# An attention and gated feed-forward kernel: the planner's release times of the output-weight preparation, 40 units earlier

## The chip, the cores and the metric

The kernel runs on one core of one Trainium2 chip. The metric is device time in microseconds (us) for one execution, measured without the profiler; the profile shows another, single execution. Engines go by the profile's names: PE is the TensorE matmul, PEld its weight load, DVE the VectorE, ACT the ScalarE, POOL the GpSimd, SP the SyncE, whose queue issues nearly every transfer (DMA).

## The reference

For 8 batches and 8 heads (576 positions, 64 wide) windowed attention is computed; its output, as 4608 tokens of 512 features, goes through a gated feed-forward layer with 1536 hidden features.

```python
scores = np.where((rel >= 0) & (rel < 128), scale * q @ k.T + slope * -abs(rel), -1e9)
x = (softmax(scores) @ v)                        # as 4608 x 512 tokens
gate = 1.0 / (1.0 + np.exp(-(x @ w_gate)))
val = x @ w_val
return (gate * val @ w_out).astype(np.float32)
```

## The kernel before

Every engine's program is written out by a planner. `Graph.add` takes an operation with its engine, an assumed cost, the keys that it reads and writes, a priority `want` and a `release`, before which the planner doesn't start it. `Graph.order` plays a list schedule on these assumed costs and emits the operations sorted by their planned start. On the chip nothing is timed: each engine runs its list in this order and waits on semaphores. So a `release` sets only where an operation stands in the lists, in the planner's own microseconds.

The work has three stages. First, attention of 32 head pairs, and the first four blocks of 128 hidden features for the first 2048 or so tokens (`ffn`, L646). Second, the **seven-product stage** (`ffn2`, L780): the gate and value products of a block as a 2x2 block matrix product with seven products in place of eight (Winograd's form). A *chunk* is one block of 128 hidden features for one group of tokens. It has seven products of six matmuls each, in the order 0, 3, 4, 1, 5, 2, 6, on three PSUM banks `bx`, `by`, `bz`. Products 4, 5 and 6 accumulate on `bx`, product 2 on `bz`, after ACT has copied out what stood there: to `low` (L201), or for product 3 to the chunk's buffer `later_hs` (L201, `p5`), and DVE has added (L787) and gated (L795). The finished chunk is stored to DRAM (`hid`). The stage runs first over groups of 2 x 384 tokens (24 chunks), then over three groups of 2 x 512 tokens (24 chunks). Third, the output product (`last`, L910), by the same form, for all five groups; it reads `hid` back (`rows_*`), builds sums of it (`csum`, L865) and splits them into pairs (`duo`).

The weights are split into a high and a low float32r part. For the output weights this is `prepare_o(n)`, n = 0 to 5: two loads of 512 KB (`wraw`), decoding (ACT L337, DVE L338 and L341), differences of the quarter blocks (L209, L210) in `tt`, splitting into `wg0` and `wtmp0`, `wtmp1` (L201 or L202, then L210), and four stores to DRAM (`stash_o`, two of 128 KB and two of 768 KB). Later `fetch_o` reads each `stash_o` back into the space of a weight tile of the second stage (`wo`, two of 896 KB), when that tile has been used for the last time.

The six preparations share `wraw`, `tt`, `wtmp0` and `wtmp1`. These last two lie in the memory of the third and fourth `later_hs` buffers:

```python
six = lambda p: T(moe, f"wtmp{p}", [P, 6, 2 * P], F32R, tag=f"h{3 + p}")
def hs(e, name="later_hs"):
    return T(moe, f"{name}{e}", [P, 2, NB] if name == "later_hs" else [P, NB], F32, tag=f"hs{e}" if e < 2 else f"h{e + 1}")
```

In most of the stage the chunks take turns on `later_hs0` and `later_hs1`. In the last group of 512 (`ends`) they take turns on all four, so there the third chunk of the group writes `later_hs2` where `wtmp0` was, and the fourth `later_hs3` where `wtmp1` was:

```python
if ends:
    for p in range(2):
        follow([("wtmp", p)] + [("hs", 2 + p, j) for j in range(2)])
...
e = turns[0] % (4 if ends else 2)
```

`rows_hs0` and `rows_h3` of the last stage are loaded into the memory of `later_hs0` and `later_hs2`, once the store of the chunk there has landed. All these transfers stand in one list on SP, which issues them in order and waits for each one's condition before the next.

When a preparation may be planned is set by two constants, `OUT0` and `OSTEP`:

```python
for n in range(NFC // 2):
    prepare_o(n, 2.0e6 + n, OUT0 + OSTEP * n)
```

Of the kernel before, what the change touches and what calls it, by code (L numbers as in the profile page):

```python
# [39 lines left out]
KEEP2 = 3  # L40
NPB, NST, NPT, NBOTH = 8, 9, 3, 2
P0, PSTEP = 120.0, 56.0
OUT0, OSTEP = 470.0, 36.0
TRI = 3
VDELAY = 1
VHEAD = 11
# [1048 lines left out]
```

## Time and profile before

| | |
|---|---|
| time, three runs | 987.4, 987.62, 988.33 us; median 987.62 us |
| the profiled execution's own time | 988.12 us |
| its span, first to last instruction | 986.4 us |
| mean granted TensorE clock | 0.994 |
| busy: PE, DVE, ACT, POOL | 98%, 80%, 52%, 13% |
| seven-product stage, L780 | about 304 to 724 us of the span |
| output product, L910 | 723.96 us to the end |

The table says which engine is busy, not which wait ends last; that is read in the rows below. The 1.72 us between span and own time lie before the first and behind the last instruction.

### The profile page before, as it was taken

Reading aid. Unit: us, or ns where it says so; the run is one execution under the profiler, and the core shown is the slowest. Engines: PE = TensorE matmul, PEld = TensorE weight load, DVE = VectorE, ACT = ScalarE, POOL = GpSimd, SP = SyncE. Lnnn points to the kernel's source line nnn. Section 1 sums busy time; section 2 is a strip of 40 time slices with the busy share of each in tenths; the row PEclk is TensorE's granted clock in tenths of the full one; section 3 lists DMA queues with packets and bytes.
Section 4 is the critical chain, followed back from the end, with each engine's and each line's share of the span. In section 5 each row is a group of like instructions: output and inputs, shape, how many; then the busy total and the mean of one; then the engine's idle time right before and its main releaser. Section 6 shows DMA issues by size and latency. Waiting matters only on the chain.

```text
span 986.4 us, 18539 instructions
## 1 busy us (share of the span) xinstructions
PE 962.8 (98%) x6592; PEld 835.3 (85%) x6592; DVE 793.7 (80%) x2014; ACT 509.4 (52%) x1324; POOL 126.8 (13%) x221
## 2 busy tenths in 40 slices
PE   8999999999999999999999999995999999999998
PEld 7677888888879999999988888884888888889998
DVE  8999989898978998867866867755498977877783
ACT  8999877878745454334533533522344433333341
POOL 3434343343320000000020000000000000000000
PEclk9999999999999999999999999997999999999999
DMA  8778768877645444233382373393986435162601
GB/s 299 259 235 305 234 214 293 276 230 243 206 135 177 141 141 135 98 139 134 131 302 118 124 292 150 107 355 119 393 294 194 157 109 192 60 197 80 193 17 64
DMA packets 82077, 186.03 MB, mean 189 GB/s; under 512 B 7744, under 2 KB 36800, under 8 KB 81984
## 3 DMA queue, kind: packets, MB, share of 16 engines
q1 hardware_dynamic: 81840, 184.71, 54.2%
q8 instruction: 52, 0.85, 0.4%
q14 instruction: 41, 0.34, 0.1%
q10 hardware_dynamic: 144, 0.13, 0.0%
HBM read 122.95 MB, written 61.87 MB: 187 GB/s over the span
## 4 chain that ended last, share of the span: by engine, by line
PE 64%; DVE 2%; DMA 1%; issue 0%; ACT 0%; ACTq 0%
PE mm L780 38%; PE mm L910 26%; DMA hid<-later_hs 0%; DVE wbits L341 0%; DVE mm L787 0%; DMA stash_o<-wtmp 0%; DVE w2s L210 0%; DMA stash_o<-wg 0%; DVE later_hs L795 0%; DVE later_hs L787 0%; ACT low L201 0%; DVE wbits L338 0%; DVE wtmp L202 0%; DVE low L743 0%; DVE later_xr L743 0%
## 5 line engine op out<-in xcount | busy, mean ns | idle before, releaser
L780 PE MATMUL mm<-xc,w2s 128*128 128x384 f32 (+1 forms) x2016 | 408.1, 364 | 12.2 <-ACT later_hs L201 9.2
L780 PEld LDWEIGHTS mm<-xc,w2s 128*128 128x128 f32 x2016 | 365.5, 189 | 54.6 <-ACT later_hs L201 9.7
L910 PE MATMUL mm<-duo,wo 128*128 128x512 f32 (+1 forms) x1260 | 258.9, 367 | 0.0
L910 PEld LDWEIGHTS mm<-duo,wo 128*128 128x128 f32 x1260 | 229.3, 188 | 29.5
L646 PE MATMUL mm<-first,first 128*128 128x512 f32 x576 | 154.0, 406 | 1.7 <-DVE first L210 1.3
L646 PEld LDWEIGHTS mm<-first,first 128*128 128x128 f32 x576 | 102.0, 188 | 25.2 <-DVE first L210 2.9
L787 DVE TENSOR_TENSOR mm<-mm,low 128x384 f32<-128x384 f32 (+1 forms) x96 | 60.1, 628 | 66.0 <-PE mm L780 65.4
L791 ACT ACTIVATE sg<-mm 128x384 f32<-128x384 f32 (+1 forms) x96 | 52.2, 545 | 114.9 <-PE mm L780 65.1
L201 ACT COPY low<-mm 128x384 f32<-128x384 f32 (+1 forms) x94 | 50.2, 534 | 82.5 <-PE mm L780 70.8
L475 ACT ACTIVATE pb<-pb,st 128x128 f32<-128x128 f32 x216 | 84.5, 396 | 5.4 <-DVE st L471 5.1
L571 POOL TENSOR_SCALAR_AFFINE_SELECT pt<-early_h 128x384 f32<-128x384 f32 x96 | 51.7, 558 | 112.6 <-ACT early_h L201 102.3
L571 POOL TENSOR_SCALAR_AFFINE_SELECT pt<-early_xr 128x384 f32<-128x384 f32 x96 | 51.9, 563 | 52.0 <-ACT early_xr L201 48.3
L463 DVE COPY_PREDICATED mm<-early_h,mm 128x256 f32<-128x256 int32 (+1 forms) x144 | 50.1, 389 | 4.0 <-PE mm L446 3.8
L471 DVE CUSTOM_DVE_ANT_0 pb<-mm,early_h 128x128 f32<-128x128 f32 x216 | 51.0, 280 | 0.0
L517 PEld LDWEIGHTS mm<-pt,vr 64*64 64x64 f32 x924 | 37.5, 133 | 9.1 <-issue 3.5
L795 DVE SCALAR_TENSOR_TENSOR later_hs<-sg,later_hs 128x384 f32<-128x384 f32 (+1 forms) x48 | 31.5, 656 | 15.7 <-ACT sg L791 15.7
L201 ACT COPY later_hs<-mm 128x512 f32<-128x512 f32 (+1 forms) x45 | 24.1, 535 | 36.9 <-PE mm L780 20.8
L475 ACT ACTIVATION_READ_ACCUMULATOR pb<-pb,st 128x1 f32 x216 | 41.5, 192 | 0.0
L517 PE MATMUL mm<-pt,vr 64*64 64x192 f32 (+2 forms) x924 | 41.4, 285 | 0.0
L201 ACT COPY early_xr<-mm 128x384 f32<-128x384 f32 (+3 forms) x76 | 32.9, 446 | 14.0 <-PE mm L517 9.8
L787 DVE TENSOR_TENSOR later_hs<-mm,later_hs 128x384 f32<-128x384 f32 (+1 forms) x48 | 29.8, 620 | 11.6 <-ACT sg L791 5.3
L553 DVE TENSOR_SCALAR pb<-pb,st 128x128 f32<-128x128 f32 x162 | 38.2, 286 | 0.2
(138 smaller groups left out, 1222.3 us busy)
## 6 DMA issues: line engine op xcount, KB each, us to landing
hid<-later_hs SPq DMA_DIRECT2D x24, 512.0 KB, 4.6
wo<-stash_o SPq DMA_DIRECT2D x12, 896.0 KB, 7.7
vr<-in_v_dram SPq DMA_DIRECT2D x32, 288.0 KB, 4.8
hid<-later_hs SPq DMA_DIRECT2D x24, 384.0 KB, 2.8
stash_o<-wtmp SPq DMA_DIRECT2D x12, 768.0 KB, 4.1
wraw<-in_moe_w_gate_dram SPq DMA_DIRECT2D x16, 512.0 KB, 4.6
wraw<-in_moe_w_val_dram SPq DMA_DIRECT2D x16, 512.0 KB, 4.2
kr<-in_k_dram SPq DMA_DIRECT2D x11, 576.0 KB, 4.7
```

What stands on the lines that cost most here:

```text
L201: g.add("ACT", act_cost(n, psum), lambda: nc.scalar.copy(out(), src()), reads, writes, want, release=release, slack=slack, ways=[("DVE", d ...
L463: g.add("DVE", dve_cost((a1 - a0) * P, psum=True), lambda b=b, a0=a0, a1=a1: nc.vector.copy_predicated(quads(b)[:, a0:a1, 1:3], before[:, ...
L471: g.add("DVE", 0.21, lambda: nc.vector.tensor_tensor_reduce(pb()[:, e], sp[b][:, a, D:D + P], relm[u.p][:, w], op0=ALU.add, op1=ALU.min, s ...
L475: g.add("ACT", 0.39, lambda: nc.scalar.activation(pb()[:, e], pb()[:, e], AF.Exp, bias=st()[:, e:e + 1], scale=-1.0, accum_out=st()[:, 3 + ...
L517: nc.tensor.matmul(mm[WORK[h]][e * D:(e + 1) * D, a - e * S - cuts[h]:b - e * S - cuts[h]], vraw(u)[r * D:r * D + D, c], seen, start=first ...
L553: g.add("DVE", 0.19, lambda args=args: nc.vector.tensor_scalar_mul(*args()), [(kst, 6)], [(kpb, e)], want, port=True, ways=[("ACT", 0.3, F ...
L571: nc.gpsimd.affine_select(pt(u)[:, f0:f0 + 2 * n - 1:2, :], both(), [[0, n], step], cmp, 0.0, base=0, channel_multiplier=mult)
L646: nc.tensor.matmul(mm[s][:, 0:wd], w.tile(kind, wi, i)[:, c * P:(c + 1) * P], xpart(x, c)[:, 0:wd], start=(k == 0 and c == 0), stop=(k == ...
L780: nc.tensor.matmul(mm[b][:, 0:N2], w.tile2(i, wp)[:, wk, c * P:(c + 1) * P], combo(k, xp, N2)[:, c], start=(start and c == 0 and j == 0), ...
L787: g.add("DVE", dve_cost(N2, psum=True), lambda: nc.vector.tensor_tensor(o(), bk(b)(), a(), op=ALU.add), [("mm", b), *reads] if okeys else ...
L791: g.add("ACT", act_cost(N2, psum=True), lambda: nc.scalar.activation(sg[h](), bk(b)(), AF.Tanh, scale=0.5), [("mm", b)], [("sg", h)], F)
L910: nc.tensor.matmul(mm[b][:, 0:N2], wo2(2 * q + m, wp)[:, k, j * P:(j + 1) * P], duo(xp)[:, m], start=(k in (0, 3, 1) and q == 0 and m == 0 ...
```

## The change

One constant changes. The planner may start the six preparations at 430, 466, ... 610 of its own microseconds, where it could at 470, 506, ... 650. No operation is added or removed; their places in the lists change.

```diff
-OUT0, OSTEP = 470.0, 36.0
+OUT0, OSTEP = 430.0, 36.0
```

**SP, the end of the seven-product stage.** These rows stand in SP's list before, around the stores of the fifth and the loads and stores of the sixth preparation. `stash_o_113` is the fifth, `stash_o_114` the sixth; `wtmp_5938` is `wtmp0`; `hid_142` and `hid_137` are the stores of the first and second chunk of the last group, `hid_122` of the third.

```order
L206 DMA hid_142<-later_hs_4329 128x1024
L206 DMA stash_o_113<-wg_5876 128x256
L206 DMA stash_o_113<-wtmp_5938 128x1536
L206 DMA stash_o_113<-wtmp_5947 128x1536
L206 DMA wo_6926<-stash_o_110 128x1792
L206 DMA wo_6929<-stash_o_110 128x1792
L206 DMA hid_137<-later_hs_4357 128x1024
L206 DMA wraw_215<-in_moe_w_out_dram 128x1024
L206 DMA wraw_221<-in_moe_w_out_dram 128x1024
L206 DMA stash_o_114<-wg_5876 128x256 x2
L206 DMA stash_o_114<-wtmp_5938 128x1536
L206 DMA stash_o_114<-wtmp_5947 128x1536
```

The same place of the changed kernel, where `wtmp_5663` is `wtmp0`:

```order
L206 DMA hid_142<-later_hs_4329 128x1024
L206 DMA stash_o_114<-wtmp_5663 128x1536
L206 DMA stash_o_114<-wtmp_5673 128x1536
L206 DMA wo_6948<-stash_o_110 128x1792
L206 DMA wo_6951<-stash_o_110 128x1792
L206 DMA hid_137<-later_hs_4357 128x1024
L206 DMA wo_7014<-stash_o_111 128x1792
L206 DMA wo_7016<-stash_o_111 128x1792
```

Between the first two chunks' stores the sixth preparation's `wtmp` stores stand where the fifth's stood, and behind the second chunk's no preparation is left. The preparations two to five move in the same way, each about to where the one before it in number was.

**ACT, the place of the first preparation.** It stands in the last two groups of 384 now, where no preparation of output weights was. `low` and `later_hs` are the copies out of PSUM that PE waits for; `mm` is a bank.

```order
 L201 COPY later_hs_4357<-mm_74 128x384
 L201 COPY low<-mm_72 128x384
+L337 ACTIVATE wbits_417<-wraw_215 128x512
 L201 CAST xc_4380<-later_xr 128x2x384
 L791 ACTIVATE sg_782<-mm_73 128x384
+L337 ACTIVATE tt<-wraw_221 128x512
 L201 COPY low<-mm_75 128x384
```

Two decodings that wait for loads now stand in front of copies that PE waits for.

**DVE, the last chunks of the stage.** The rows of the changed kernel around the first sum for the output product; `later_hs_4357` is the sixth chunk's buffer, `later_hs_6989` the seventh's.

```order
L795 SCALAR_TENSOR_TENSOR later_hs_4357<-sg_782,mm_72 128x512
L795 SCALAR_TENSOR_TENSOR later_hs_4357<-sg_888,later_hs_4357 128x512
L865 TENSOR_TENSOR csum_7201<-rows_xr,rows_hs_7171 128x1024
L865 TENSOR_TENSOR rows_xr<-rows_xr 128x1024
L787 TENSOR_TENSOR mm_74<-mm_74,low 128x512
L787 TENSOR_TENSOR later_hs_6989<-mm_73,later_hs_6989 128x512
```

Before, the first of the two L865 stood one chunk later, behind the seventh chunk's last gate, and the second behind all chunks. In SP's list the load of `rows_hs0` went with it, from behind the sixth chunk's store to behind the fifth's.

## Rows read from the trace of the kernel before

**Rows 1.** The page, busy time of the engines, share of the span, instructions.

```profile
PE 962.8 (98%) x6592; PEld 835.3 (85%) x6592; DVE 793.7 (80%) x2014; ACT 509.4 (52%) x1324; POOL 126.8 (13%) x221
```

**Rows 2.** Timeline of PE, 300 to 740: start, length, work, idle before and releaser.

```profile
320.05 54.79 PE L780 MATMUL mm<-xc,w2s 128*128 128x384 f32 x312 [0.38 <-DVE later_hs L787]
376.09 7.58 PE L780 MATMUL mm<-xc,w2s 128*128 128x384 f32 x42 [1.25 <-DVE later_hs L787]
384.19 287.35 PE L780 MATMUL mm<-xc,w2s 128*128 128x384 f32 x1398 [0.52 <-ACT low L201]
672.21 1.66 PE L780 MATMUL mm<-xc,w2s 128*128 128x512 f32 x6 [0.68 <-ACT low L201]
683.11 41.01 PE L780 MATMUL mm<-xc,w2s 128*128 128x512 f32 x168 [9.23 <-ACT later_hs L201]
723.96 16.26 PE L910 MATMUL mm<-duo,wo 128*128 128x512 f32 x71
```

**Rows 3.** Timeline of all engines, 655 to 700, the rows ahead of the long wait.

```profile
672.06 0.67 ACT L337 ACTIVATE wbits<-wraw 128x512 f32<-128x512 f32 x1
...
679.13 2.11 SPq L206 DMA_DIRECT2D stash_o<-wtmp  x2
...
682.47 0.58 ACT L201 COPY later_hs<-mm 128x512 f32<-128x512 f32 x1 [7.39 <-DMA stash_o<-wtmp]
```

**Rows 4.** Stretches: PE, PEld, DVE, ACT, POOL busy (instructions), granted clock, DMA share, GB/s.

```profile
440.00:460.00 20.00, 20.00 (x117) 20.00 (x116) 16.50 (x26) 10.22 (x19) 0.00 (x0) 1.00 0.47 165
480.00:500.00 20.00, 20.00 (x92) 16.90 (x92) 19.97 (x27) 11.27 (x19) 4.76 (x4) 1.00 0.64 226
...
683.00:688.00 5.00, 4.89 (x12) 3.88 (x13) 2.08 (x3) 1.23 (x3) 0.00 (x0) 0.50 0.15 59
688.00:691.00 3.00, 3.00 (x13) 2.46 (x12) 1.44 (x3) 1.14 (x3) 0.00 (x0) 0.87 0.37 110
```

**Rows 5.** Groups by line and shape: busy us, mean ns, idle before.

```profile
L910 PE MATMUL mm<-duo,wo 128*128 128x512 f32 x756 | 171.5, 389 | 0.0
```

**Rows 6.** Timeline of SP's transfers, 560 to 730: start, time to issue.

```profile
651.40 2.59 SPq L206 DMA_DIRECT2D stash_o<-wtmp  x2
...
658.22 1.20 SPq L206 DMA_DIRECT2D wraw<-in_moe_w_out_dram  x2
```

**Rows 7.** Transfers issued 651 to 651.8: count, KB, us to landing.

```profile
stash_o<-wtmp SPq DMA_DIRECT2D x1, 768.0 KB, 7.8
```

**Rows 8.** Timeline of SP's transfers, 439 to 440.5.

```profile
439.76 0.52 SPq L206 DMA_DIRECT2D hid<-later_hs  x1
```

**Rows 9.** Instructions that touch `wraw`: landing times of its loads.

```profile
DMA to landing us min/median/max: 3.3/4.5/10.3
```

**Rows 10.** Timeline of ACT, 432 to 482.

```profile
449.03 0.48 ACT L201 COPY low<-mm 128x384 f32<-128x384 f32 x1 [0.53 <-ACT later_hs L201]
...
452.16 0.48 ACT L201 COPY low<-mm 128x384 f32<-128x384 f32 x1 [0.65 <-PE mm L780]
```

**Rows 11.** Transfers issued 688 to 691, a store.

```profile
hid<-later_hs SPq DMA_DIRECT2D x1, 512.0 KB, 7.5
```

**Rows 12.** Timeline of DVE, 728 to 733, past the seam to the output product.

```profile
731.36 1.23 DVE L865 TENSOR_TENSOR csum<-rows_hs,rows_h 128x1024 f32<-128x1024 f32 x1 [0.17 <-DMA rows_h<-hid]
732.51 1.22 DVE L210 TENSOR_TENSOR duo<-csum,duo 128x1024 fp32r<-128x1024 f32 x1
```

**Rows 13.** The page, costliest groups: busy us, mean ns, idle before and releaser.

```profile
L787 DVE TENSOR_TENSOR mm<-mm,low 128x384 f32<-128x384 f32 (+1 forms) x96 | 60.1, 628 | 66.0 <-PE mm L780 65.4
```

**Rows 14.** Timeline of SP's transfers, 698 to 712.

```profile
699.73 0.32 SPq L206 DMA_DIRECT2D hid<-later_hs  x1
...
706.52 0.32 SPq L206 DMA_DIRECT2D hid<-later_hs  x1
709.98 0.37 SPq L206 DMA_DIRECT2D rows_hs<-hid  x1
```

**Rows 15.** Transfers issued 709 to 711.

```profile
rows_hs<-hid SPq DMA_DIRECT2D x1, 512.0 KB, 6.8
```

## The prediction

> **What bounds the kernel.** The page comes first: PE is busy for 962.8 of 986.4 us [rows 1], so no more than 23.6 us can be had from its idle time, and only a stretch in which PE stands matters. PE's timeline shows where that is within reach of the change. From 384.19 to 671.54 (384.19 + 287.35) it runs without a break, waits 0.68, does six matmuls, waits 9.23 for an ACT copy into `later_hs`, does 168, and goes over to L910 at 723.96 [rows 2]. The timeline of all engines names the reason: the loads of the sixth preparation are issued at 658.22 [rows 6], its decoding starts at 672.06, its `wtmp` stores are issued from 679.13 on, and the copy into `later_hs2`, which lies on `wtmp0`, waits 7.39 us for them to land [rows 3]. So the wait that ends last is that for the last preparation to leave its buffer. [...]
>
> **What the wait costs now.** From 671.54 to 723.96 are 52.42 us for 6 + 168 = 174 matmuls [rows 2]. L910's matmuls of the same 512 columns never wait and take 171.5 / 756 = 0.2269 us each [rows 5]; 174 of them are 39.48. So 52.42 - 39.48 = **12.94 us** are lost here: 9.91 in the two waits, 3.03 in matmuls slower than that step.
>
> **The change part by part.** *What it removes.* In SP's new list the sixth preparation's `wtmp` stores take the place of the fifth's, between the stores of the first two chunks of the last group. The fifth's were issued from 651.40 on [rows 6], and the first landed 7.8 later [rows 7], at 659.2. With a product of 6 x 0.2269 = 1.361 us and L910 starting at 723.96 - 12.94 = 711.02, the first product that needs the copy into `later_hs2` (the third chunk's sixth, 36 products ahead of L910 in PE's new list) starts at 662.0. The copy takes 0.58 [rows 3], so it has 2.2 us to spare. On ACT no preparation stands in front of it any more. The wait of 9.23 goes, and the clock need not fall. The wait of 0.68 came from two products on one bank in direct succession, with a copy to be made between; that order was the planner's way around the late buffer, and in the new list another product stands between them. All 12.94 go.
>
> *What it adds.* Preparations two to five stand about where one to four stood, in 476 to 650, in which PE never waits [rows 2]. Those I cost at nothing, with the same cover as before: evictions that leave DVE idle. The first goes to a new place, among the last chunks of 384. There DVE is busy for 16.50 of 20 us (440 to 460) and PE for all 20; in its old place, 480 to 500, DVE was busy for 19.97 and PE still for all 20 [rows 4]. So a fuller DVE than this stretch will have has been borne by PE: cost 0. Bound from above: the three waits in the 384 chunks, where weights are prepared as well, 0.38, 1.25 and 0.52 [rows 2]; I take the largest, 1.25.
>
> Its two loads queue on SP behind the store at 439.76 [rows 8], so they are issued at about 440.3 and land after 3.3 to 10.3 us, in the median 4.5 [rows 9], at 443.6 to 450.6. ACT reaches the first decoding behind the copy that ends at 449.03 + 0.48 = 449.51 [rows 10]: there by then in the median case, 1.1 us late in the worst. Behind it ACT has to make the copy of 452.16 [rows 10], for which PE waits. ACT's longest wait of rows 3 shows what happens then: nothing else runs on ACT for 7.39 us. [...]
>
> *What comes next.* DVE's new list has the first sum for L910, `csum0`, directly behind the sixth chunk's last gate, one chunk earlier than before, and a second sum behind it. `csum0` needs the load of `rows_hs0`, which SP issues when the fifth chunk's store has landed. Store five and store six are one chunk apart, 42 x 0.2269 = 9.53 us, and DVE asks for `csum0` at store six. A store issued behind a pair of `wo` loads into an idle queue landed after 7.5 [rows 11], and a load of this size takes 4.5 in the median [rows 9]: 12.0, so DVE waits 2.5 and then sums twice at 1.15 (732.51 - 731.36, [rows 12]): free 4.8 us after store six. PE needs the seventh chunk's adds before that chunk's seventh product, which starts 6 x 1.361 = 8.17 after the sixth chunk's end; the gate ahead and the adds are four evictions of 0.63 [rows 13], leaving 8.17 - 2.5 = 5.6. It fits by 0.8. The upper bound is the queue as it was: store at 699.73, load issued only at 709.98 [rows 14], 6.8 to landing [rows 15], 17.05 in all; DVE is then free 9.8 after store six, 4.2 late. So 0 to 4.2. The `wo` loads were crowded behind the late chunk before and will come one per chunk, so I stand at the low end and take 0.3.
>
> At the seam, PE's new list wants the split of `csum1` as ninth product of L910, 8 x 1.361 = 10.9 us after its start, one product earlier than before. `csum1` ran at 731.36, 7.40 after the seam, as soon as `rows_h` landed [rows 12]. Behind it now stand a further difference, another sum and the split's own subtraction: four at 1.15 make 12.0, 1.1 late. But `rows_h` now has one transfer of 512 KB less in front of it, which pays that back. Bounds 0 and 1.1; I take 0.3.
>
> *Sum.* 12.94 - 0.3 - 0.3 = 12.3 us. Against the profiled execution's own 988.12 (span 986.4 and 1.72 around it) that gives 975.8; it was 0.5 above the median of 987.62, so **975.3 us** is forecast, 1.25% faster.
>
> **The rivals.**
> *The sums come early and wait* (10 in 100). `rows_hs0` lands as in the crowded queue, and DVE, held at `csum0`, keeps the seventh chunk's adds from PE. For it: the margin is 0.8 us. Against: the queue is emptier. With 4.2 in place of 0.3 the time is 979.2.
> *The hand-over only moves* (9). The sixth preparation's stores come a chunk later than its slot, say because one of its steps waits. They then land at 668.7, the copy ends at 669.3, PE waits 7.3 us from 662.0 and loses clock in proportion, 7.3 x 12.94 / 9.91 = 9.5: 984.8. Against: the fifth preparation kept this slot.
> *The loads of the first preparation hold ACT* (3; the slower one). The place is ACT's decoding at 449.5. To end over 2 us above 987.62, PE must lose 12.3 + 2 = 14.3, by the ratio above a wait of 11 us: a landing after 449.5 + 11 = 460.5, 20 us after the issue, about twice the longest of this kernel [rows 9]. Then 989.6 and more.
> *Nothing changes* (2). The saved time is given back in the last stage, if L910's first sums and not PE set its pace: then L910 starts earlier and ends as before, at 987.6. Against: in 171.5 us of its 512-column matmuls PE never waits [rows 5].
>
> **How the numbers follow.** The forecast has the remaining 76 in 100. Its own range goes from 974.7 (all 12.94) less the spread of the runs (988.33 - 987.62 = 0.7), 974.0, to 977.5, where 2 us are given back. With the first rival, 979.2, and something for the first preparation, the range is 974.0 to 980.0; it leaves out 14 in 100. A measurement of this kernel can tell about 0.2%, 2 us, from no change. Faster by more: 76 + 10 + 9 = 95; within: 2; slower: 3.
>
> **What would show it.** Right: no wait of PE for `later_hs` near 660 to 685; granted clock 1.00 throughout 640 to 720; L910 starting near 711.6; the sixth preparation's `wtmp` stores issued near 651 and the copy into `later_hs2` without a wait for a transfer. The first preparation: ACT's L337 near 449.5 with little idle before it, and PE busy for all of 440 to 465. The sums: a DVE idle of about 2.5 us before the first L865 near 693, and no PE wait at 700. Wrong: a PE wait of several us in 655 to 702, or a busy DVE and an idle PE in the first 25 us of L910.

## The result and the profile after

The changed kernel takes **978.81 us** in the median of 4 runs (978.13 to 979.75), the kernel before 987.98 beside it (987.40 to 990.28): ratio 0.9904, 95% interval [0.9885, 0.9922]. That is 9.2 us less; 12.3 were forecast, so the time lies 3.5 above the forecast and inside the range. Its profiled execution takes 978.13, where 975.8 was forecast, with a span of 976.4.

PE's timeline of the changed kernel, from the end of the 384 chunks to the end of the program (start, length, work, idle before and releaser):

```profile
385.51 192.18 PE L780 MATMUL mm<-xc,w2s 128*128 128x384 f32 x978 [0.66 <-ACT low L201]
577.90 135.20 PE L780 MATMUL mm<-xc,w2s 128*128 128x512 f32 x594 [0.21 <-DVE later_hs L787]
712.94 11.49 PE L910 MATMUL mm<-duo,wo 128*128 128x512 f32 x50
725.15 247.73 PE L910 MATMUL mm<-duo,wo 128*128 128x512 f32 x1210 [0.71 <-DVE duo L210]
```

The waits of 0.68 and 9.23 of [rows 2] are gone; L910 starts at 712.94 in place of 723.96. A new wait of 0.71 stands 12.21 after its start, and a small one of 0.21 at 577.90; PE waited at neither place before. The timeline of SP and ACT around the old wait:

```profile
652.68 3.21 SPq L206 DMA_DIRECT2D stash_o<-wtmp  x2
655.98 2.30 SPq L206 DMA_DIRECT2D wo<-stash_o  x2
658.37 1.09 SPq L206 DMA_DIRECT2D hid<-later_hs  x1
...
662.09 0.60 ACT L791 ACTIVATE sg<-mm 128x512 f32<-128x512 f32 x1 [1.53 <-DVE mm L787]
662.58 0.58 ACT L201 COPY later_hs<-mm 128x512 f32<-128x512 f32 x1
```

The sixth preparation's `wtmp` stores go out at 652.68, ahead of the second chunk's store; in [rows 3] they went out at 679.13, behind it. The copy at 662.58 is the one into `later_hs2`: no bracket, so ACT had no idle time in front of it, against 7.39 us before. The first of the stores took 9.0 us to land, so it was there at 661.7, 0.9 ahead of the copy. The stretches (columns: PE, PEld, DVE, ACT, POOL busy us, then granted clock, DMA share, GB/s):

```profile
660.00:680.00 20.00, 20.00 (x90) 16.57 (x89) 6.94 (x10) 6.95 (x12) 0.00 (x0) 1.00 0.95 347
680.00:700.00 20.00, 20.00 (x90) 16.57 (x89) 8.89 (x12) 5.92 (x10) 0.00 (x0) 1.00 0.73 253
...
440.00:460.00 20.00, 20.00 (x117) 20.00 (x116) 19.41 (x31) 11.96 (x22) 1.44 (x2) 1.00 0.62 212
```

The clock is 1.00 where [rows 4] had 0.50 and 0.87. In 440 to 460, where the first preparation went, DVE rose from 16.50 to 19.41 of 20 us, and PE still is busy for all 20.

**Where the time went.** Marks of PE's timelines, the two kernels with every profile that was taken of them (us; the last two rows are differences of those above):

| | before | before, second | changed | changed, second | changed, third |
|---|---|---|---|---|---|
| start of L780 | 303.87 | 306.25 | 304.80 | 304.59 | 304.08 |
| start of L910 | 723.96 | 726.61 | 712.94 | 713.57 | 712.49 |
| end (span) | 986.4 | 989.1 | 976.4 | 976.9 | 979.2 |
| L780 to L910 | 420.09 | 420.36 | 408.14 | 408.98 | 408.41 |
| L910 to the end | 262.44 | 262.49 | 263.46 | 263.33 | 266.71 |

The programs are the same up to about 440, so the start of L780 is a matter of the execution: it moves by 2.4 us between two profiles of the kernel before. L780 to L910 is the gain: 420.2 to 408.5 in the mean, 11.7 us. L910 to the end is what is given back: 1.0, 0.9 and 4.3 us.

### The profile page after: what moved, and what is told of

It reads as the page before. It is cut to its first block, busy times and chain, and to the rows that moved or that the text cites. A ratio compares the mean times of both kernels' runs of the same rounds, so it can differ in the third digit from the quotient of the medians.

```text
span 976.4 us, 18551 instructions
## 1 busy us (share of the span) xinstructions
PE 961.3 (98%) x6592; PEld 833.4 (85%) x6592; DVE 790.1 (81%) x2009; ACT 512.5 (52%) x1326; POOL 129.3 (13%) x224
## 4 chain that ended last, share of the span: by engine, by line
PE 60%; DVE 3%; DMA 3%; issue 1%; ACT 0%; SPq 0%; DVEq 0%; ACTq 0%
PE mm L780 35%; PE mm L910 25%; DMA hid<-later_hs 1%; DMA later_xr<-xs 1%; DVE mm L787 1%; DVE xc L210 0%; DMA rows_h<-hid 0%; DVE later_hs L795 0%; DVE later_xr L743 0%; DVE w2s L210 0%; DVE later_hs L787 0%; DVE csum L865 0%; DVE duo L210 0%; DVE wbits L341 0%; DVE duo L202 0%
## 5 line engine op out<-in xcount | busy, mean ns | idle before, releaser
L780 PE MATMUL mm<-xc,w2s 128*128 128x384 f32 (+1 forms) x2016 | 405.4, 362 | 2.9 <-DVE later_hs L787 2.2
L780 PEld LDWEIGHTS mm<-xc,w2s 128*128 128x128 f32 x2016 | 363.6, 188 | 44.6 <-DVE later_hs L787 4.1
L910 PE MATMUL mm<-duo,wo 128*128 128x512 f32 (+1 forms) x1260 | 259.2, 367 | 0.7 <-DVE duo L210 0.7
L910 PEld LDWEIGHTS mm<-duo,wo 128*128 128x128 f32 x1260 | 229.2, 188 | 30.7 <-DVE duo L210 1.1
L787 DVE TENSOR_TENSOR later_hs<-mm,later_hs 128x384 f32<-128x384 f32 (+1 forms) x48 | 29.8, 621 | 12.9 <-ACT sg L791 7.3
```

The costliest lines, as they stand in the source:

```text
L780: nc.tensor.matmul(mm[b][:, 0:N2], w.tile2(i, wp)[:, wk, c * P:(c + 1) * P], combo(k, xp, N2)[:, c], start=(start and c == 0 and j == 0), ...
L787: g.add("DVE", dve_cost(N2, psum=True), lambda: nc.vector.tensor_tensor(o(), bk(b)(), a(), op=ALU.add), [("mm", b), *reads] if okeys else ...
L910: nc.tensor.matmul(mm[b][:, 0:N2], wo2(2 * q + m, wp)[:, k, j * P:(j + 1) * P], duo(xp)[:, m], start=(k in (0, 3, 1) and q == 0 and m == 0 ...
```

## The experiments

All medians and ratios in one table. Each four rows were taken on one chip together, with runs of the kernel before among them (medians 988.89, 988.17 and 989.15 us). Two numbers name a kernel by its release and step.

| run | median us (lowest to highest, runs) | ratio to before, 95% interval |
|---|---|---|
| changed again, 430/36 | 979.31 (977.25 to 980.14, 4) | 0.9900 [0.9887, 0.9913] |
| last early, 470/28 | 976.66 (975.45 to 976.80, 4) | 0.9874 [0.9861, 0.9886] |
| first early, 430/44 | 989.00 (987.14 to 992.94, 12) | 1.0004 [0.9993, 1.0016] |
| two buffers, 470/36 | 984.08 (982.88 to 984.44, 5) | 0.9948 [0.9935, 0.9961] |
| sum late, 430/36 | 979.36 (977.58 to 981.30, 6) | 0.9906 [0.9888, 0.9924] |
| load order, 430/36 | 977.57 (976.21 to 978.89, 5) | 0.9887 [0.9870, 0.9904] |
| release 450/36 | 975.78 (974.68 to 976.80, 4) | 0.9868 [0.9850, 0.9886] |
| last early and load order, 470/28 | 978.64 (977.58 to 980.76, 6) | 0.9900 [0.9883, 0.9918] |
| before again, 470/36 | 988.75 (987.45 to 991.99, 12) | 0.9999 [0.9989, 1.0010] |
| changed, third time, 430/36 | 981.02 (977.35 to 981.97, 6) | 0.9911 [0.9895, 0.9927] |
| release 450/36 again | 975.85 (974.94 to 980.74, 5) | 0.9875 [0.9856, 0.9894] |
| release 460/36 | 985.15 (982.46 to 986.90, 6) | 0.9958 [0.9943, 0.9974] |

### Which preparation is it: the first or the last?

The theory: only the last preparation's place in the lists counts, through the buffer under its `wtmp0`. The rival: the gain comes from the first preparation's new place, or from all of them being spread otherwise. Two kernels move one end alone.

```diff
-OUT0, OSTEP = 470.0, 36.0
+OUT0, OSTEP = 470.0, 28.0
```

> Releases 470, 498, ... 610: the first preparation stays where it was, the sixth is as early as in the changed kernel. Theory (the wait was that for the sixth preparation to leave the buffer of later_hs2): no PE wait for later_hs near 660 to 685, clock 1.00 from 640 on, L780 from its last 384 chunks to the seam as short as in the changed kernel (327.4 us from the mark at 384 to 386 to L910, give or take 1.5), time 977 to 980. Rival (the gain is that of spreading the preparations over the 384 chunks, where DVE has room): the five preparations crowd the 512 chunks, most of the wait or others like it remain, and the time stays above 983.

```diff
-OUT0, OSTEP = 470.0, 36.0
+OUT0, OSTEP = 430.0, 44.0
```

> Releases 430, 474, ... 650: the first preparation is as early as in the changed kernel, the sixth as late as before. Theory: PE waits for later_hs again, some 5 to 10 us near 665 to 685, since the stores of wtmp stand behind the second chunk's store again, the granted clock falls to 0.5 behind it, and the time is 983 to 989. Rival (the early ones make the gain): 978 to 981 and no long wait. It also gives the price of the first preparation alone: theory 0 to 0.5 us between the marks at 430 and 500.

And the changed kernel once more, for the spread:

> The changed kernel once more, for its time and for how far one profile stands from the next. In its first profile the first L780 matmul starts at 304.80 us, against 303.87 before, in a stretch in which both programs are the same. If that is only how executions vary, this profile puts the mark somewhere between 303.5 and 305.5 without regard to the kernel, and the median is 978 to 979.5, 0.9% under before. If the change made the early part slower, the mark is again at or above 304.7. The wait at the seam to L910 (0.71 us for DVE's duo) and the DVE wait of 2.7 us at the first csum are to come again within 0.5 us, since they follow from the order.

The changed kernel takes 979.31 again, and L780 starts at 304.59. Of the two waits that were to come again within 0.5 us, that at the seam (the passage from L780 to L910) did, with 0.54; that at the first sum did not, with 4.38.

With the last preparation alone early the time is 976.66, just below the expected range: all of the gain and more. With the first alone early it is 989.00, as before. PE's timeline of the latter, then ACT's copy and SP's stores:

```profile
677.33 1.66 PE L780 MATMUL mm<-xc,w2s 128*128 128x512 f32 x6 [0.68 <-ACT low L201]
688.25 40.60 PE L780 MATMUL mm<-xc,w2s 128*128 128x512 f32 x168 [9.26 <-ACT later_hs L201]
```
```profile
687.61 0.58 ACT L201 COPY later_hs<-mm 128x512 f32<-128x512 f32 x1 [7.42 <-DMA stash_o<-wtmp]
```
```profile
684.24 2.11 SPq L206 DMA_DIRECT2D stash_o<-wtmp  x2
```

The two waits are those of [rows 2] to within 0.03 us, and the copy waits for the same store as in [rows 3]; the granted clock behind them is 0.50 in 688 to 693. So the first preparation's place, moved alone, is worth nothing either way. The lead of 470/28 over the changed kernel beside it, 2.65 us, lies between L780 and L910 in the profiles (406.34 and 408.98); 1.38 of it is a wait at the first sum and 0.57 the wait near 385, both taken up below.

### Is it the buffer?

The kernel before with one line changed, so that the last group too takes turns on `later_hs0` and `later_hs1` only. No chunk then needs the memory of `wtmp0`.

```diff
-            e = turns[0] % (4 if ends else 2)
+            e = turns[0] % 2
```

> The preparations stay at 470, 506, ... 650, but the last group's chunks take turns on later_hs0 and later_hs1 alone, so nothing needs the memory of wtmp. Theory: the long wait is gone although the sixth preparation still runs near 672 to 681; L910 starts at 711 to 713 and the clock stays at 1.00. The loads of rows_hs0 and rows_hs1 now wait for the last two chunks' stores, so PE may wait 0 to 6 us in the first 20 us of L910: time 976 to 983. Rival (the sixth preparation's own DVE and ACT work in front of the evictions holds PE): PE still waits 5 us or more near 673 to 683, and the time is 983 or more.

The time is 984.08, a little above the expected range. PE's timeline, and SP's:

```profile
458.62 251.99 PE L780 MATMUL mm<-xc,w2s 128*128 128x384 f32 x1140 [0.40 <-DVE later_hs L787]
710.46 8.32 PE L910 MATMUL mm<-duo,wo 128*128 128x512 f32 x36
724.11 1.22 PE L910 MATMUL mm<-duo,wo 128*128 128x512 f32 x2 [5.33 <-ACT duo L201]
726.56 252.25 PE L910 MATMUL mm<-duo,wo 128*128 128x512 f32 x1222 [1.23 <-DVE duo L210]
```
```profile
682.12 0.32 SPq L206 DMA_DIRECT2D stash_o<-wtmp  x1
```

The sixth preparation is as late as before (682.12), yet PE runs without a break from 458.62 to L910: the wait is the buffer's, shown. What the kernel saves there it loses at the start of L910, where DVE waits 4.85 us for a load into `rows_ar` and the granted clock is 0.83 in 720 to 740: 271.94 us from L910 to the end in place of 262.44. So in this kernel the seam costs 9.5 us, where the prediction allowed it 0 to 1.1 in the changed one.

### How much late costs how much

Two releases between the two kernels. The change is the constant 450 or 460 in place of 430.

> Releases at 450, 486, ... 630, half way between the two kernels. The sixth preparation's wtmp stores stand directly behind the second chunk's store, one chunk later than in the changed kernel and about 20 us earlier than before it. Theory (the wait is set by when these stores land): issued about 659.5, landed about 667.3 with the 7.8 us of a landing, the copy into later_hs2 done about 667.9, PE asks for it from about 662 (up to 1.4 later where two products are exchanged): a PE wait of 4.5 to 6 us, and with the loss of clock 5 to 8 us: 984 to 987. Rival 1 (only a place behind all other work costs anything; the landing is short as the queue is empty): 978 to 981. Rival 2 (the wait is all or nothing): 988 to 989.

The expectation failed: 975.78, the fastest kernel of the study, and no wait. SP's row, and ACT's two copies behind it:

```profile
661.04 2.11 SPq L206 DMA_DIRECT2D stash_o<-wtmp  x2
```
```profile
666.48 0.59 ACT L201 COPY low<-mm 128x512 f32<-128x512 f32 x1 [4.80 <-PE mm L780]
666.96 0.59 ACT L201 COPY later_hs<-mm 128x512 f32<-128x512 f32 x1
```

The stores were issued later than in the changed kernel, at 661.04 (about 659.5 was expected). But the planner, which knows the buffer to be late, had put other products first, so ACT comes to the copy at 666.96 and not at 662, 43.0 us ahead of L910 where the changed kernel has 50.4; and a landing took 5.3 us there in the median, not 7.8. The first store was there at 666.3, so the margin is 0.7 us, and enough.

> Releases at 460, 496, ... 640. PE's list is that of the kernel before around the late buffer; the loads of the sixth preparation stand ten us earlier on SP, its decoding on ACT one copy earlier (behind the copy that ran at 667.50 before, in place of 671.58). Theory (the wait is set by when the last preparation's stores land): decoding 4.0 us earlier, so a PE wait of 9.2 - 4.0 = 5.2 us in place of 9.2, lost clock in proportion (5.2 x 12.94 / 9.91 = 6.8 us in all), 6 less than before: 981 to 983. Rival (all or nothing by the place behind the second chunk's store): 987 to 989, or 976 to 978.

The time is 985.15, 4.0 less than before where 6 to 8 were expected. ACT's decoding and copy:

```profile
669.46 0.67 ACT L337 ACTIVATE wbits<-wraw 128x512 f32<-128x512 f32 x1
...
679.67 0.58 ACT L201 COPY later_hs<-mm 128x512 f32<-128x512 f32 x1 [6.93 <-DMA stash_o<-wtmp]
681.55 0.58 ACT L201 COPY later_hs<-mm 128x512 f32<-128x512 f32 x1 [1.29 <-DMA stash_o<-wtmp]
```

Counted from the start of L780 (304.54 here), the decoding is 364.92 after it, before 672.06 - 303.87 = 368.19: 3.27 earlier, not 4.0. PE's wait is 6.73 in place of 9.23, 2.50 shorter, and L780 to L910 is 416.74, 3.35 shorter. So the wait is neither all nor nothing: it follows the time of the preparation. The rest of the miss is the seam, 985.2 - 721.28 = 263.92 us from L910 to the end, 1.5 more than before.

### What is given back: two suspects

The prediction left two costs open: `csum0`, made one chunk earlier on DVE, and `csum1` with its split at the seam. In the changed kernel DVE shows (timeline, first sum, then the seam):

```profile
698.01 1.23 DVE L865 TENSOR_TENSOR csum<-rows_xr,rows_hs 128x1024 f32<-128x1024 f32 x1 [2.71 <-DMA rows_hs<-hid]
```
```profile
720.34 1.23 DVE L865 TENSOR_TENSOR csum<-rows_hs,rows_h 128x1024 f32<-128x1024 f32 x1 [4.88 <-DMA rows_h<-hid]
721.60 1.23 DVE L865 TENSOR_TENSOR rows_hs<-rows_xr,rows_hs 128x1024 f32<-128x1024 f32 x1
722.74 1.22 DVE L865 TENSOR_TENSOR csum<-rows_ar 128x1024 f32<-128x1024 f32 x1
723.88 3.49 DVE L210 TENSOR_TENSOR duo<-csum,duo 128x1024 fp32r<-128x1024 f32 x3
```

*The first sum.* Undone alone, by a release of its own:

```diff
-            g.add("DVE", dve_cost(n, two=True), lambda: nc.vector.tensor_tensor(o(), a(), b(), op=op), reads, writes, F, port=True, ways=[way])
+            g.add("DVE", dve_cost(n, two=True), lambda: nc.vector.tensor_tensor(o(), a(), b(), op=op), reads, writes, F, port=True, ways=[way], release=690.0 if (t, writes) == (0, [("csum", 0)]) and len(reads) == 2 else 0.0)
```

> The changed kernel with the first sum for the output product (csum0) put back where it stood before the change, behind the seventh chunk's last gate. Theory (the early sum costs between nothing and 1.4 us, by how late rows_hs0 lands in the execution): no PE wait for later_hs near 702, L910 starting 39.4 us after the last matmul before the hand-over, and a median 0 to 1.4 us below that of the changed kernel (979 in the first measurement), so 977.9 to 979.3. Rival (the early sum is harmless or helps, since the second sum behind it then has to be made later, at the seam): the median is the same or up to 1 us higher, 979.3 to 980.3, with a longer DVE chain after 712.

979.36: as the changed kernel. The early sum is no large part of what is missing. The trace shows in outline what the rival of this expectation said: the loss comes at the seam instead, where PE waits 1.49 us in place of 0.71, with 0.32 for an add just ahead, and L910 to the end takes 264.3 us. In the second profile of the changed kernel, though, the early sum did what the prediction's first rival said, in small. DVE, then PE:

```profile
698.66 1.23 DVE L865 TENSOR_TENSOR csum<-rows_xr,rows_hs 128x1024 f32<-128x1024 f32 x1 [4.38 <-DMA rows_hs<-hid]
```
```profile
702.40 11.33 PE L780 MATMUL mm<-xc,w2s 128*128 128x512 f32 x48 [1.38 <-DVE later_hs L787]
```

DVE waits 4.38 in place of 2.71 for the load, and PE 1.38 for DVE. The margin of 0.8 us that the prediction worked out is real: 1.7 more us use it up. In the other two profiles PE does not wait there.

*The seam.* `csum1` waits for `rows_h`, whose load stands ahead of the second of `rows_ar` in the new list, and behind it in the old. This was put back by a higher `want`:

```diff
-                     reads, [("raw", h, c, q)], F + 0.1 * ((0, 3), (1, 2))[h][c], n / 2, True)
+                     reads, [("raw", h, c, q)], F + 0.1 * ((0, 3), (1, 2))[h][c] + (0.05 if (t, h, c, q) == (0, 1, 1, 1) else 0.0), n / 2, True)
```

> The changed kernel with the load of rows_h behind the second load of rows_ar again, as before the change, so that the sum made from rows_ar stands ahead of the one made from rows_h. Theory (the seam costs 0.7 to 1.0 us since csum1 waits 4.7 to 4.9 us for rows_h, whose load waits for a store): the PE wait of 0.5 to 0.7 us at the ninth product of L910 is gone or under 0.2, L910 to the end is 262.4 to 262.8 us in place of 263.3 to 263.5, the median 0.5 to 1.0 lower than the changed kernel's: 978.3 to 978.8. Rival (the split of csum1 is late because of the sums in front of it on DVE, whichever load comes first): the wait stays at 0.5 or more and the median within 0.4 of the changed kernel's.

> Releases at 470, 498, ... 610, with the same change of the load order of rows_h. Theory (the hand-over by the last preparation's place alone; the seam as in the run on load order): no long PE wait in 640 to 705, none above 0.2 at the ninth product of L910, a median 0.5 to 1.0 below the 976.7 of these releases alone: 975.7 to 976.2. Rival (the lead of these releases over the changed kernel was the difference between executions and not a property of the order): 978 to 979.

Both missed. With the order of old, PE's wait at the seam is longer, 1.47 us with 430/36 and 1.75 with 470/28 (0.51 there without this edit): in these two lists PE's ninth product of L910 needs a split that stands second of three on DVE (the three run from 722.14 on in the first of the two kernels, and PE goes on at 724.54). DVE takes the sums of `rows_ar` first there and waits 4.43 us for their load. The time of the first, 977.57, is lower than the changed kernel's all the same; its L780 to L910 is 406.96, without the wait of 0.6 us near 385 that all profiles of the changed kernel have. Up to that place the two programs are the same, so this says nothing of the edit. The second is slower than 470/28 alone, 978.64 to 976.66, but the two were not taken together and their intervals overlap.

What the loads wait for is seen in SP's timeline. The changed kernel, then the kernel before:

```profile
705.83 0.37 SPq L206 DMA_DIRECT2D rows_hs<-hid  x1
706.29 0.89 SPq L206 DMA_DIRECT2D wo<-stash_o  x2
707.24 0.47 SPq L206 DMA_DIRECT2D hid<-later_hs  x1
713.13 0.37 SPq L206 DMA_DIRECT2D rows_ar<-hid  x1
715.98 0.37 SPq L206 DMA_DIRECT2D rows_h<-hid  x1
```
```profile
716.04 0.32 SPq L206 DMA_DIRECT2D hid<-later_hs  x1
716.42 0.46 SPq L206 DMA_DIRECT2D rows_hs<-hid  x1
724.15 0.89 SPq L206 DMA_DIRECT2D rows_ar<-hid  x2
725.09 0.46 SPq L206 DMA_DIRECT2D rows_h<-hid  x1
```

`hid` here is the seventh chunk's store. Before, it stood ahead of the load into `rows_hs1` and was issued in the moment its gate ended on DVE, 7.92 us before L910. In the new list the load into `rows_hs1` stands in front of it, and that load, issued at 705.83, had to wait until the sixth chunk's store (issued at 695.53) had landed, after 10.3 us. The seventh's gate ended at 704.84; its store went out at 707.24, 2.4 late and 5.70 before L910. `rows_h` lies in the buffer that this store empties and was issued 8.7 after it, in the moment in which it had landed.

> The changed kernel a third time. If the start of L780 (304.6 to 304.8 in two profiles) and the wait of 0.6 for ACT's low near 385 belong to the program, they are here again, and the median is 978.8 to 979.4. If they belong to the execution, L780 starts between 303.3 and 304.2 or that wait is gone in this profile. L910 waits 0.5 to 0.7 for duo in either case.

The third profile of the changed kernel shows how far this goes. SP, DVE and PE:

```profile
705.94 0.42 SPq L206 DMA_DIRECT2D hid<-later_hs  x1
712.68 0.37 SPq L206 DMA_DIRECT2D rows_ar<-hid  x1
714.57 0.37 SPq L206 DMA_DIRECT2D rows_h<-hid  x1
```
```profile
721.83 1.22 DVE L865 TENSOR_TENSOR csum<-rows_hs,rows_h 128x1024 f32<-128x1024 f32 x1 [6.83 <-DMA rows_h<-hid]
```
```profile
724.18 0.73 PE L910 MATMUL mm<-duo,wo 128*128 128x512 f32 x2 [0.66 <-ACT duo L201]
726.64 249.03 PE L910 MATMUL mm<-duo,wo 128*128 128x512 f32 x1210 [1.72 <-DVE duo L210]
```

Here `rows_h` took 7.2 us to land, against 4.3 and 3.9 in the first two profiles. `csum1` starts 9.34 after L910 in place of 7.40, PE waits 2.38 in two pieces, and the granted clock is 0.83 in 720 to 730. L910 to the end is 266.71, 4.3 more than before.

The median, 981.02, and the wait at the seam lie above what was expected. The start of L780 is 304.08 and so belongs to the execution, but the wait for `low` near 385 is here again (0.57).

> Releases at 450, 486, ... 630 once more, beside the changed kernel in the same call. If its lead of 3 us over the changed kernel is real, the median is 975 to 976.8 and below that of the changed kernel by 2 to 4. If it was the choice of executions, the two differ by less than 1.

Again 975.85, beside 981.02 for the changed kernel: the lead is real (the upper end of its interval, 0.9894, lies just below the lower end of the other, 0.9895). Its L780 to L910 is 406.33, its seam 262.84 with no wait of PE. In its SP list, too, a load into `rows_hs` stands ahead of the seventh chunk's store, but the gate ends at 702.27 and the store goes out at 702.65, 7.71 before L910. Yet `rows_h` lands no sooner: it is issued at 711.59 and takes 5.9 us, so it lands 7.1 after the start of L910, where the changed kernel had 7.3. DVE:

```profile
715.90 1.22 DVE L865 TENSOR_TENSOR csum<-rows_ar 128x1024 f32<-128x1024 f32 x1 [1.89 <-DMA rows_ar<-hid]
...
718.37 1.22 DVE L865 TENSOR_TENSOR csum<-rows_hs,rows_h 128x1024 f32<-128x1024 f32 x1
719.50 3.49 DVE L210 TENSOR_TENSOR duo<-csum,duo 128x1024 fp32r<-128x1024 f32 x3
```

The sums of `rows_ar` stand ahead of `csum1` here and the splits directly behind it. `csum1` starts 8.01 after L910, later than in the changed kernel, and PE does not wait; in the run with the late first sum it starts 6.12 after L910, and PE waits 1.49. So what stands behind the landing in the lists counts as well as the landing, and no run separates the two.

> The kernel before, once more, with a profile of its own. It tells what of the 12.94 us is a property of the program. Theory: the stretch from the last matmul ahead of the long wait to L910 is 52.4 us again (within 0.5), with a wait of about 9.2 for the copy into later_hs2; the start of L780 differs by up to 1 us from the 303.87 of the first profile, for a reason ahead of the change. Rival (the wait is a matter of the execution): a stretch that is over 2 us shorter or longer.

The kernel before waits 0.67 and 9.28 again, L780 to L910 takes 420.36. But from the first wait to L910 it is 51.26 us and not 52.42, outside the 0.5 that were allowed, since the matmuls after the wait lost less: 1.65 + 39.66 = 41.31 for 174, 1.83 above the full step where [rows 2] had 3.03.

## Why the prediction was right, and where its size was off

**What bounds the kernel, and what the change removes: right.** The wait was for the sixth preparation to leave `wtmp0`; it goes when that preparation alone is early, stays when it is not, shrinks with it, and goes too when the buffer is taken away. In the profiled execution the 174 matmuls ahead of L910, counted back in the trace, take 39.47 us: 52.42 - 39.47 = 12.95 against the 12.94 of the sum. The stores went out at 652.68 (651 was written) and the clock stayed at 1.00. The copy into `later_hs2` came at 662.58 without a wait. The landing ahead of it took 9.0 us and not 7.8; by the prediction's own working 1.7 us were to spare in place of 2.2.

One caution comes from the second profile of the kernel before: there the same term is 51.26 - 39.47 = 11.8. The 3.03 us of slow clock were those of one execution; the waits of 9.9 are the part that repeats.

**The first preparation at no cost: right.** The loads went out at 441.67, ACT came to the decoding at 450.75 and found them there (no bracket):

```profile
450.75 0.68 ACT L337 ACTIVATE wbits<-wraw 128x512 f32<-128x512 f32 x1
451.33 0.82 ACT L201 CAST xc<-later_xr 128x768 fp32r<-128x768 f32 x1
```

From the 600th matmul of the 384 chunks to the first of 512, counted in the trace, are 71.01, 71.00 and 70.98 us in the changed kernel, 70.77 and 71.19 in the one before. So whether a decoding that waits for its load would hold the copies behind it on ACT was not put to the test at this place. No other run tests it: with release 460 ACT does nothing while the copy into `later_hs` waits 6.93 us for a store, but the copy behind it then waits 1.29 us for a store of its own, so nothing that was ready is seen to be held. The same holds for the 7.39 us of [rows 3], from which the prediction argued: there the next copy waited 1.25 us for a store.

Preparations two to five were put at nothing; the one wait of PE in their stretch is that of 0.21 at 577.90, which two of the three profiles have.

**The first sum: right in mechanism.** DVE waited 2.71, 4.38 and 1.71 for `rows_hs0` in the three profiles (2.5 was written). Taken at 0.3, it cost PE 0, 1.38 and 0. The 0.63 us of an eviction in that sum was a mean over 384 and 512 columns [rows 13]; the adds here take 0.68 to 0.70, but back to back one starts 0.60 behind the other, so the margin stands.

**The seam: the step that was mis-sized.** The prediction said that the split would be 1.1 us late and that `rows_h`, having "one transfer of 512 KB less in front of it", would pay this back, and took 0.3 within 0 and 1.1. The delay was as worked out: 12.0 us from L910's start to the end of the split were written, PE went on at 12.21. What failed is the refund: `csum1` started 7.40 after L910 in the first profile, just where it stood before. In the changed kernel's first profile `rows_h` did not wait for what is ahead of it in the DMA queue, but for its buffer: it was issued at 715.98, when the seventh chunk's store of 707.24 had landed after 8.7 us, and in the new list that store stands behind a load which itself waits. The prediction listed where `rows_hs0` went on SP, and not `rows_hs1`. Measured: 1.0, 0.9 and 4.3 us, so the third broke the bound of 1.1; there the landing itself took 3 us longer. That the held store is the cause of what was lost is argued from these times, not tested, and the 450/36 run shows that a store on time does not bring `rows_h` earlier by itself.

With 11.7 us gained in L780 in the mean and 2.0 given back here, 9.7 are left; the medians of the three measurements differ by 9.2, 9.6 and 8.1. The 11.7 are 1.2 short of 12.94, since the second profile of the kernel before lost less clock and one of the changed kernel waited at the first sum. The time of 978.81 is nearer to the 979.2 of the first rival than to the forecast, but it came of these terms together and not of that rival; and the range holds two of the three measurements, not the third, 981.02.

**Left open.** The wait of 0.5 to 0.7 us for `low` near 385 is there in eight of the fourteen profiles: in all of the changed kernel and of the one before, with the late first sum, with 470/28 and the load order, and with 460/36. The other six do not have it, though the programs are the same up to there. The traces show it one step further back. ACT in the changed kernel, then with the load order and 430/36:

```profile
384.59 0.48 ACT L201 COPY later_hs<-mm 128x384 f32<-128x384 f32 x1 [2.35 <-DMA hid<-later_hs]
```
```profile
383.19 0.48 ACT L201 COPY later_hs<-mm 128x384 f32<-128x384 f32 x1 [0.93 <-DMA hid<-later_hs]
```

The copy in front of that into `low` waits for a chunk's store, issued at 379.75 and 379.76. It landed after 4.8 us in the first and 3.4 in the second, after 4.6 to 4.8 in all eight and 3.3 to 3.4 in all six. Why it lands later in some is open. And the repair of the seam itself, the load into `rows_hs1` behind the seventh chunk's store in the changed kernel, was not tried.

**A better release.** 450/36 is the fastest, 975.8 us in two measurements, 12.4 and 13.3 below the kernel before. No theory of the study foresaw that it beats the changed kernel. In the profiles its lead lies in L780 (406.3 against 408.5 in the mean, of which some 0.6 is the wait near 385) and behind it (263.0 against 264.5).

## What to carry to other kernels

A buffer that two phases share makes the last user of the first phase the gate for the second (here 9.23 us of PE's time): ask for its last store's landing and for the moment at which the engine's own list asks for the buffer, both, since a planner moves the second along with the first (450 against 430). When a stall is removed, list every load and store whose place changed on the queue at the seam behind it (here a store went out 2.4 us late, behind a load that waited), and ask of each what it must wait for and what stands on the engine behind its landing. Here 11.7 of the 12.9 us that were computed came, and the seam took 0.9 to 4.3 of them back. Settings in a planner's units are worth a scan: 430, 450, 460 and 470 gave 979 to 981, 976, 985 and 989 us.

## What the runs showed of the hardware

- The same 384 KB store, issued 74.7 to 75.7 us after the start of L780 in fourteen profiles, landed after 3.3 to 3.4 us in six and after 4.6 to 4.8 in eight, and never in between.
- The same 512 KB load of `rows_h` at the same place of the same program landed after 3.9, 4.3 and 7.2 us in three executions.
- Short waits went with a loss of clock in one execution and without it in three. In the third profile of the changed kernel waits of 0.66 and 1.72 stand 0.7 us apart, the granted clock is 0.83 in 720 to 730, and L910 to the end is 4.3 us longer than before for 2.4 us of waits. One wait of 0.71 in the first profile left the clock at 1.00, and so did one of 1.47 and one of 1.75 in the two runs with the load order.
- Program and data being the same up to there, the start of L780 came between 303.87 and 306.25 in the five profiles of the two kernels, and between 303.37 and 308.16 in all fourteen. In the second profile of the kernel before, the latest of the five, the granted clock was 0.51 in 38 to 45, in the first 1.00. The ends of these two profiles of the kernel before, 986.4 and 989.1, differ by 2.7 us; L780 to L910 within one execution differs by 0.27 there and by up to 0.84 in the three of the changed kernel.
